# A new hand-set order for all five engine queues of a fused gated-attention and two-matrix feed-forward kernel

## The chip, the cores and the metric

The kernel runs on one core of one Trainium2 chip. The metric is device time in microseconds (us): the median over several executions. A profile is taken of one more execution; its own time stands beside its span, which runs from the first to the last instruction of the program.

## What is computed

The reference has two parts. The first is a gated linear attention over 4 batches, 8 heads, 768 tokens and 48 channels; the second is a feed-forward layer over the 3072 tokens with 384 channels in and out and 1024 inside.

```python
f = 1.0 / (1.0 + np.exp(-f_logit))
for t in range(S):
    state = f[:, :, t, :, None] * state + np.einsum('bhd,bhe->bhde', k[:, :, t], v[:, :, t])
    y[:, :, t] = np.einsum('bhd,bhde->bhe', q[:, :, t], state)
...
g = np.maximum(x @ w1, x @ w2)
return (g @ w_out).astype(np.float32)
```

Inputs and the output are float32. The kernel multiplies in bfloat16 and uses max(h1, h2) = relu(h1 - h2) + h2, so that the output is relu(x (w1 - w2)) w_out + x (w2 w_out).

## The kernel before

The work is cut into 12 spans of 256 tokens: span s is window s // 4 of batch s % 4, so spans s and s + 4 of one batch hang together through the state. Two neighbouring tokens share a partition, and a span is two chunks of 64 partitions.

Nothing schedules the kernel but a list written out by hand, ORDER. It has one word for each step. A word is a letter for the step, the span (and a part after the point), a letter for the engine where there is a choice (a ScalarE = ACT, v or w VectorE = DVE, p GpSimd = POOL, s SyncE = SP) and, after @, the PSUM bank that the step writes or reads (some steps take two banks, that one and the next). The loop at the end of the kernel emits the steps in the order of the list; each engine runs its own words in that order and waits where a word needs another's result, a free bank or a free buffer. The words, with the lines of their instructions:

- L (L115), W (L126, L130): loads by SP. The inputs of a span are four transfers (f, k, q, v) into slots of a pool of 25; Wa, Wb and Wo bring w1, w2 and w_out in halves into slots that are reused for inputs later.
- E, F, G (L192, L196, L200; ACT): the gate's exponentials and logarithm. e (L203): the sum over a token pair. C (L207, L210; TensorE = PE): running sums. X, Z (L217, L222; ACT): their exponentials. i, j (L226, L230): k and q of the even tokens. K, Q (L237, L240): the scaled k and q in bfloat16. V (a copy, L104): v in bfloat16.
- t, u (L257; PE): transposes of K's and Q's result. U (L104): their copy out of PSUM. A (L274; PE): products of k and q; m (L282; DVE): the same under the mask. D (L358; PE): what a span adds to the state; n, N (L375 to L380): the state's update. S (L314; PE): the part of y that comes from the first chunk's state; z (L330): a small read behind it; y (L314, L342; PE): the rest of y; Y (L104): its copy to bfloat16.
- d (L398; PE): x (w1 - w2), six products of 128x128 by 128x256 for each word. r (L407 on ACT, L409 on DVE): relu. o (L424; PE): the output product, eleven products of 128x128 by 128x384. b (L104): its copy out of PSUM into the tile ob. O (L442): the store of a span in one transfer of 384 KB; P (L436): of a part of it.
- ws (L485): w1 - w2 by quarters; wc (L104), wt (L459; PE), wx (L104): cast, transpose and copy of w2 by quarters; wo (L104): cast of w_out by quarters; wm (L475; PE): the product w2 w_out in three parts, wn (L104): its copy.

PE uses three tile shapes: 64x64 in A, S, y and D, 64x128 in t and u, 128x128 in all others. Counted along ORDER, neighbouring PE words differ in shape 64 times.

Of the kernel before, what the change touches and what calls it, by code (L numbers as in the profile page):

```python
# [17 lines left out]


ORDER = """  # L20
Lf0s@12 Lk0s@13 Lq0s@14 Lv0s@15 E0 Lf1s@16 F0 G0 e0v Lk1s@12 i0v C0@0 j0v X0 Lq1s@17 Z0 K0v V0a Q0v
t0@0 Lv1s@13 u0@0 E1 D0@2 Wb0s U0v@0 F1 n0.0v A0.0@0 e1p G1 Wa0s n0.1v S0@4 Wb1s A0.1@2 z0 Wa1s i1p
m0.0v@0 C1@6 Wo0s Z1 Wo1s j1v X1 V1a K1v Lf2s@16 Q1v t1@6 wc0a m0.1v@2 u1@6 D1@0 wc1a U1v@6 y0 n1.0v
n1.1v A1.0@6 Y0a@4 N1.1w S1@2 ws0p m1.0v@6 A1.1@0 wt0@4 z1 m1.1v@0 wt1@5 Lf3s@17 ws1p wx0a@4 d0.0@6
wx1a@5 y1 wc3v d0.1@7 wc2v Y1v@2 wt2@5 r0.0a@6 wt3@4 ws2v d1.0@2 Lq2s@0 ws3p d1.1@3 wx2v@5 d1.2@6
Lk2s@1 wx3v@4 d0.2@0 r1.0v@2 wo2a wo3p d0.3@1 Lv2s@2 wo0a wo1p d1.3@7 r0.1v@0 E2 wm0@2 Lk3s@8 F2
r1.1v@6 wm2@3 E3 e2p Lq3s@16 G2 C2@6 F3 j2v wm1@7 Lv3s@17 wn2a@3 e3v X2 C3@3 Z2 i2v o0.0@0 wn0a@2
Lf4s@9 K2v wn1a@7 V2a Q2v oz0.0@0 t2@6 Lf5s@1 X3 D2@4 N0.1v G3 u2@6 n2.0v o1.0@2 b0.0a@0 i3p U2v@6
Lk4s@0 n2.1v j3v A2.0@6 Lq5s@2 b1.0a@2 A2.1@4 K3p o0.1@0 m2.0v@6 Z3 V3a Lv4s@10 m2.1v@4 S2@6 E4 D3@2
z2 Q3v Lq4s@8 t3@4 F4 y2 u3@4 G4 e4p Lk5s@16 o1.1@1 b0.1a@0 U3v@4 Y2a@6 i4p E5 n3.0v Lf7s@9 n3.1v  # L30
C4@0 b1.1v@1 d2.0@4 X4 Z4 A3.0@2 K4p Lv5s@1 A3.1@6 F5 d2.1@5 m3.0v@2 G5 d2.2@0 Lk7s@17 r2.0a@4
m3.1v@6 e5p S3@2 d2.3@1 V4a z3 C5@4 j4v Lq7s@0 y3 X5 Q4v Z5 t4@6 Y3a@2 D4@4 r2.1v@0 N2.1p Lf6s@10
u4@6 i5p d3.0@2 n4.0v d3.2@0 U4v@6 Lf8s@8 d3.1@3 j5v d3.3@1 r3.0a@2 N4.0w Lk6s@11 N3.1p o2.0@6 n4.1v
K5v E7 Lq11s@3 r3.1a@0 Q5v t5@2 A4.0@4 b2.0a@6 V5p A4.1@0 u5@2 m4.0v@4 Lq6s@2 o2.1@6 U5a@2 m4.1v@0
O0s Lv7s@1 D5@4 F7 A5.0@0 S4@2 n5.0v o3.0@7 Lk9s@9 m5.0v@0 e7p G7 E6 N5.0p z4 b2.1v@6 Lv6s@16 F6
n5.1v y4 N4.1v G6 j7v A5.1@4 S5@0 e6p Y4a@2 o3.1@6 m5.1v@4 Lf9s@10 z5 i7v j6v C6@4 C7@5 Lq9s@6
b3.0v@7 X6 d4.0@2 i6p Z7 b3.1v@6 y5 X7 K6v Z6 O1s d4.1@3 Lk8s@7 Y5a@0 K7v d4.2@4 r4.0a@2 Lv11s@11
Q6v d5.0@0 V7a d4.3@5 Q7v t6@2 O3s r4.1a@4 t7@6 u6@2 u7@6 d5.1@1 U6v@2 O2s E8 d5.2@4 F8 U7v@6 D7@2
Lv8s@8 d5.3@5 r5.0a@0 e8p n7.0v o4.0@6 N7.0w E9 V6p Lv9s@0 n7.1v r5.1v@4 Lq8s@10 N5.1p A6.0@2
b4.0a@6 D6@0 m6.0v@2 A6.1@4 C8@6 o4.1@7 Z8 n6.0v X8 m6.1v@4 N6.0p Lf10s@16 G8 A7.0@2 n6.1v b4.1a@7  # L40
A7.1@4 S7@0 m7.0v@2 F9 Lk10s@1 o5.0@7 G9 N7.1v m7.1v@4 i9p Lf11s@2 o5.1@6 b5.0a@7 z7 O4s S6@4
b5.1a@6 y7 z6 e9v O5s y6 Lq10s@17 N6.1v Y7a@0 j8v C9@6 j9v Y6a@4 d7.0@0 Lk11s@4 i8v Z9 d7.2@2 Q8v
Lv10s@5 X9 d7.1@1 V8a K9v d6.0@6 r7.0a@0 d7.3@3 K8v d6.1@7 r7.1a@2 Q9v d6.2@0 E10 t9@4 r6.0v@6 t8@2
u9@4 F10 u8@2 d6.3@1 U8v@2 E11 o7.0@6 r6.1a@0 U9v@4 D8@7 b7.0a@6 A8.0@4 A9.0@0 n8.0v V9a A9.1@2
m8.0v@4 N8.0p o6.0@7 F11 m9.0v@0 G11 V11a o7.1@6 j11v b6.0a@7 m9.1v@2 e10p V10a D9@7 e11p A8.1@2
S8@0 n9.0v o6.1@4 m8.1v@2 z8 N9.0w j10v C10@7 S9@2 i11p Z10 y8 z9 b7.1v@6 Q10p y9 b6.1v@4 O7s Y8a@0
O6s C11@6 X10 Y9v@2 d8.2@0 X11 G10 d8.0@4 K11v Z11 d9.0@2 i10v d9.2@6 K10p d9.1@3 d8.1@5 r9.0a@2
d9.3@7 Q11p r8.0v@4 d8.3@1 r9.1a@6 t10@2 t11@4 u10@2 u11@4 o9.0@6 U10v@2 U11a@4 r8.1v@0 D11@7
b9.0a@6 A10.0@4 A11.0@2 n11.0v D10@6 m10.0v@4 N11.0p A11.1@0 o8.1@7 m11.0v@2 A10.1@4 n10.0v m11.1v@0
S11@2 N10.0p o8.0@6 z11 m10.1v@4 S10@0 y11 b8.0v@6 z10 y10 Y11a@2 o9.1@6 Y10a@0 d10.0@0 b9.1v@6  # L50
d10.2@2 b8.1v@7 O9s d10.1@1 O8s d10.3@3 r10.0a@0 d11.2@6 d11.0@4 r10.1a@2 d11.3@7 d11.1@5 o10.1@2
r11.0v@4 r11.1a@6 o10.0@3 o11.0@6 b10.0v@3 b10.1v@2 O10s o11.1@7 b11.0a@6 P11.0s o11.2@6 b11.1v@7
P11.1s b11.2a@6 P11.2a
"""


# [491 lines left out]
```

## Time and profile before

| what | value |
|---|---|
| median of 3 runs (lowest, highest) | 139.84 us (139.73, 140.19) |
| the profiled execution's own time | 139.43 us |
| its span | 137.6 us |
| granted clock of TensorE | 1.000 |
| DVE busy | 104.5 us, 165 instructions |
| ACT busy | 81.2 us, 120 instructions |
| POOL busy | 43.6 us, 53 instructions |
| moved by DMA | 28.68 MB, mean 208 GB/s |

The profile gives each engine's busy time, the span in 40 slices with the busy share of each in tenths, groups of instructions with their mean duration and the idle time before them, and the chain of work that ended last, followed back from the last instruction. The loads are spread over the first 92 us: SP issued the last one (v of span 10) at 89.46 us. PE's instructions can all be told apart by line, and since PE runs its words in the order of the list, every word's start and end can be read from the timeline: the first product of w2 and w_out (wm0) starts at 30.08 us, the last product of PE (o11.2) ends at 134.61 us.

### The profile page before, as it was taken

The numbers are of one execution on the slowest core, as the hardware profiler recorded it, in microseconds if no ns is written. First come the engines' busy times: TensorE is split into PE (matmuls) and PEld (weight loads), VectorE is DVE, ScalarE is ACT, GpSimd is POOL, SyncE is SP. The second block draws the span as 40 slices with busy tenths as digits, with TensorE's granted clock in tenths as the row PEclk, the third lists the DMA queues.
The fourth block names the chain that finished last, engine by engine and source line by source line (L and its number), as shares of the span: only waits on it lengthen the run. The fifth ranks groups of instructions, "written<-read, shape, count | busy, mean of one in ns | idle before, by whom it ended". The sixth has DMA issues, their size and how long they took to land.

```text
span 137.6 us, 5766 instructions
## 1 busy us (share of the span) xinstructions
PE 120.9 (88%) x2575; PEld 89.7 (65%) x2575; DVE 104.5 (76%) x165; ACT 81.2 (59%) x120; POOL 43.6 (32%) x53
## 2 busy tenths in 40 slices
PE   0047397999998999999999999999999999999991
PEld 0035286775656678666787667886678876778670
DVE  5778999995897799988969994988888379620330
ACT  3646564279847883898599554988717570226110
POOL 7604119542162587017104320002814902000000
PEclk9999999999999999999999999999999999999999
DMA  4999999999999999999998799994005000005023
GB/s 107 273 261 262 368 388 377 346 257 256 270 264 251 253 252 265 254 272 317 250 296 246 261 286 260 325 283 118 5 0 225 13 2 5 5 21 213 0 114 114
DMA packets 54617, 28.68 MB, mean 208 GB/s; under 512 B 50240, under 2 KB 51648, under 8 KB 54592
## 3 DMA queue, kind: packets, MB, share of 16 engines
q1 hardware_dynamic: 54448, 28.25, 77.8%
q8 instruction: 20, 0.33, 1.0%
q10 hardware_dynamic: 144, 0.07, 0.2%
q14 instruction: 5, 0.04, 0.1%
HBM read 23.59 MB, written 4.72 MB: 206 GB/s over the span
## 4 chain that ended last, share of the span: by engine, by line
PE 65%; DMA 13%; DVE 10%; SPq 3%; ACT 3%; issue 3%; DVEq 0%
PE banks L424 28%; PE banks L398 16%; DMA slots<-in_moe_w_out_dram 10%; PE banks L342 4%; PE banks L257 4%; PE banks L274 3%; PE banks L475 3%; DMA slots<-in_f_logit_dram 3%; PE banks L314 3%; DVE at_m L282 2%; DVE slots L230 2%; SPq L126 2%; PE banks L358 2%; PE banks L207 2%; DVE trs L104 2%
## 5 line engine op out<-in xcount | busy, mean ns | idle before, releaser
L424 PE MATMUL banks<-wo,gT 128*128 128x384 bf16 (+2 forms) x200 | 35.3, 320 | 0.0
L398 PE MATMUL banks<-xT,wd 128*128 128x256 bf16 x288 | 34.2, 273 | 1.0 <-POOL wd L485 0.8
L398 PEld LDWEIGHTS <-wd 128*128 128x128 bf16 x288 | 27.0, 98 | 5.3 <-POOL wd L485 1.1
L282 DVE TENSOR_TENSOR at_m<-banks,mask 128x1024 bf16<-128x1024 f32 x24 | 28.8, 1216 | 1.6 <-PE banks L274 1.4
L424 PEld LDWEIGHTS <-gT 128*128 128x128 bf16 x200 | 19.2, 98 | 11.9
L407 ACT ACTIVATE gT<-banks 128x1024 bf16<-128x1024 f32 x15 | 15.2, 1019 | 11.1 <-PE banks L398 10.4
L203 POOL TENSOR_TENSOR e<-ell 128x384 bf16<-128x384 f32 x9 | 9.1, 1019 | 27.1 <-ACT ell L196 21.0
L424 PE MATMUL banks<-m,xT 128*128 128x384 bf16 (+2 forms) x75 | 15.9, 321 | 0.0
L409 DVE TENSOR_SCALAR gT<-banks 128x1024 bf16<-128x1024 f32 x9 | 10.9, 1219 | 6.3 <-PE banks L398 6.3
L104 DVE COPY trs<-banks 128x2048 bf16<-128x2048 bf16 x10 | 12.0, 1220 | 4.6 <-PE banks L257 4.6
L104 ACT COPY ob<-banks 128x384 f32<-128x384 f32 (+2 forms) x15 | 7.5, 506 | 13.2 <-PE banks L424 12.5
L104 ACT CAST xT<-banks 128x768 bf16<-128x768 f32 x10 | 8.0, 800 | 9.0 <-PE banks L342 8.9
L104 DVE COPY ob<-banks 128x384 f32<-128x384 f32 (+2 forms) x14 | 7.2, 540 | 7.5 <-PE banks L424 5.5
L192 ACT ACTIVATE gate<-slots 128x768 f32<-128x768 f32 x12 | 10.0, 837 | 4.1 <-DMA slots<-in_f_logit_dram 4.1
L342 PE MATMUL banks<-at_m,vb 64*64 64x128 bf16 x576 | 11.6, 224 | 0.0
L380 POOL TENSOR_TENSOR st<-tmp_s,dec 128x192 bf16<-128x192 f32 x8 | 4.1, 510 | 20.7 <-PE banks L274 12.9
L274 PE MATMUL banks<-trs 48*64 48x128 bf16 x384 | 9.9, 230 | 0.8 <-DVE trs L104 0.8
L226 POOL TENSOR_TENSOR slots<-slots,one 128x384 f32<-128x384 f32 x7 | 8.0, 1145 | 7.6 <-ACT one L200 7.0
L196 ACT ACTIVATE ell<-gate 128x768 f32<-128x768 f32 x12 | 10.1, 843 | 0.5
L207 PE MATMUL banks<-e,u_inc 128*128 128x384 bf16 x12 | 4.2, 353 | 7.0 <-DVE e L203 6.8
L230 DVE SCALAR_TENSOR_TENSOR slots<-gate,slots 128x384 f32<-128x384 f32 x12 | 8.7, 732 | 1.7 <-DMA slots<-in_k_dram 1.4
L342 PEld LDWEIGHTS <-vb 64*64 64x64 bf16 x576 | 10.0, 111 | 0.0
...
## 6 DMA issues: line engine op xcount, KB each, us to landing
...
```

Of the source, the lines that this page charges most:

```text
L104: (nc.scalar.copy if e == "a" else engines[e].tensor_copy)(out, in_)
L192: nc.scalar.activation(flat(gate[s]), flat(loaded[s]["f"]), AF.Exp, bias=0.0, scale=-1.0)
L196: nc.scalar.activation(flat(ell[s]), flat(gate[s]), AF.Ln, bias=1.0, scale=1.0)
L203: engines[e].tensor_add(pad("e", s)[:, :, 0:D], ell[s][:, :, 0, :], ell[s][:, :, 1, :])
L230: engines[e].scalar_tensor_tensor(out=even, in0=gate[s][:, :, 1, :], scalar=1.0, in1=even, op0=ALU.add, op1=ALU.mult)
L274: nc.tensor.matmul(out=ps[h * HC:(h + 1) * HC, j % 2, par, :], lhsT=t[rows, h, 0, j, par, :], rhs=t[rows, h, 1, j].rearrange("p a t -> p ( ...
L282: nc.vector.tensor_mul(at[s][:, jj].rearrange("p r j a t -> p (r j) (a t)"), banks[:, b:b + 2, :].rearrange("p r (j x) -> p (r j) x", j=2) ...
L342: nc.tensor.matmul(out=ys[s][h][cols, kt, :], lhsT=window(vb[rows, par], head, off), rhs=m[rows, head // 4, head % 2, head // 2 % 2, par, ...
L398: nc.tensor.matmul(out=ps[:, f, :], lhsT=wd[:, kt, ff * C:(ff + 1) * C], rhs=x_flat(g)[:, kt, :], start=(kt == 0), stop=(kt == KT - 1))
L407: nc.scalar.activation(dst, src, AF.Relu)
L409: nc.vector.tensor_relu(dst, src)
L424: nc.tensor.matmul(out=ps, lhsT=x, rhs=w, start=(n == 0), stop=(n == KT + FG - 1))
```

## The change

Only ORDER changes. The words of the steps are the same but for stores and engines: all words of PE (177) stay, in another order, and neighbouring ones now differ in tile shape 56 times instead of 64 (9 instead of 8 times ahead of the product of w2 and w_out, 47 instead of 56 times from there on). Other words go to other engines, the largest shifts being: V to POOL 7 times (2 before), to DVE once and to ACT 4 times (10); U to ACT 4 times (2); b to ACT 19 times (13); K and Q to POOL 4 and 3 times (3 and 2); e to DVE 6 times (3); Y to DVE 4 times (2); two quarters of ws to DVE (one before), wc all to ACT (two before). Banks and slots are renumbered to fit. Spans 7 to 10 are stored in two transfers of 192 KB (P) instead of one of 384 KB (O); three of these halves are issued by ACT.

```diff
-Lf0s@12 Lk0s@13 Lq0s@14 Lv0s@15 E0 Lf1s@16 F0 G0 e0v Lk1s@12 i0v C0@0 j0v X0 Lq1s@17 Z0 K0v V0a Q0v
-t0@0 Lv1s@13 u0@0 E1 D0@2 Wb0s U0v@0 F1 n0.0v A0.0@0 e1p G1 Wa0s n0.1v S0@4 Wb1s A0.1@2 z0 Wa1s i1p
-m0.0v@0 C1@6 Wo0s Z1 Wo1s j1v X1 V1a K1v Lf2s@16 Q1v t1@6 wc0a m0.1v@2 u1@6 D1@0 wc1a U1v@6 y0 n1.0v
-n1.1v A1.0@6 Y0a@4 N1.1w S1@2 ws0p m1.0v@6 A1.1@0 wt0@4 z1 m1.1v@0 wt1@5 Lf3s@17 ws1p wx0a@4 d0.0@6
-wx1a@5 y1 wc3v d0.1@7 wc2v Y1v@2 wt2@5 r0.0a@6 wt3@4 ws2v d1.0@2 Lq2s@0 ws3p d1.1@3 wx2v@5 d1.2@6
-Lk2s@1 wx3v@4 d0.2@0 r1.0v@2 wo2a wo3p d0.3@1 Lv2s@2 wo0a wo1p d1.3@7 r0.1v@0 E2 wm0@2 Lk3s@8 F2
-r1.1v@6 wm2@3 E3 e2p Lq3s@16 G2 C2@6 F3 j2v wm1@7 Lv3s@17 wn2a@3 e3v X2 C3@3 Z2 i2v o0.0@0 wn0a@2
-Lf4s@9 K2v wn1a@7 V2a Q2v oz0.0@0 t2@6 Lf5s@1 X3 D2@4 N0.1v G3 u2@6 n2.0v o1.0@2 b0.0a@0 i3p U2v@6
-Lk4s@0 n2.1v j3v A2.0@6 Lq5s@2 b1.0a@2 A2.1@4 K3p o0.1@0 m2.0v@6 Z3 V3a Lv4s@10 m2.1v@4 S2@6 E4 D3@2
-z2 Q3v Lq4s@8 t3@4 F4 y2 u3@4 G4 e4p Lk5s@16 o1.1@1 b0.1a@0 U3v@4 Y2a@6 i4p E5 n3.0v Lf7s@9 n3.1v
-C4@0 b1.1v@1 d2.0@4 X4 Z4 A3.0@2 K4p Lv5s@1 A3.1@6 F5 d2.1@5 m3.0v@2 G5 d2.2@0 Lk7s@17 r2.0a@4
-m3.1v@6 e5p S3@2 d2.3@1 V4a z3 C5@4 j4v Lq7s@0 y3 X5 Q4v Z5 t4@6 Y3a@2 D4@4 r2.1v@0 N2.1p Lf6s@10
-u4@6 i5p d3.0@2 n4.0v d3.2@0 U4v@6 Lf8s@8 d3.1@3 j5v d3.3@1 r3.0a@2 N4.0w Lk6s@11 N3.1p o2.0@6 n4.1v
-K5v E7 Lq11s@3 r3.1a@0 Q5v t5@2 A4.0@4 b2.0a@6 V5p A4.1@0 u5@2 m4.0v@4 Lq6s@2 o2.1@6 U5a@2 m4.1v@0
-O0s Lv7s@1 D5@4 F7 A5.0@0 S4@2 n5.0v o3.0@7 Lk9s@9 m5.0v@0 e7p G7 E6 N5.0p z4 b2.1v@6 Lv6s@16 F6
-n5.1v y4 N4.1v G6 j7v A5.1@4 S5@0 e6p Y4a@2 o3.1@6 m5.1v@4 Lf9s@10 z5 i7v j6v C6@4 C7@5 Lq9s@6
-b3.0v@7 X6 d4.0@2 i6p Z7 b3.1v@6 y5 X7 K6v Z6 O1s d4.1@3 Lk8s@7 Y5a@0 K7v d4.2@4 r4.0a@2 Lv11s@11
-Q6v d5.0@0 V7a d4.3@5 Q7v t6@2 O3s r4.1a@4 t7@6 u6@2 u7@6 d5.1@1 U6v@2 O2s E8 d5.2@4 F8 U7v@6 D7@2
-Lv8s@8 d5.3@5 r5.0a@0 e8p n7.0v o4.0@6 N7.0w E9 V6p Lv9s@0 n7.1v r5.1v@4 Lq8s@10 N5.1p A6.0@2
-b4.0a@6 D6@0 m6.0v@2 A6.1@4 C8@6 o4.1@7 Z8 n6.0v X8 m6.1v@4 N6.0p Lf10s@16 G8 A7.0@2 n6.1v b4.1a@7
-A7.1@4 S7@0 m7.0v@2 F9 Lk10s@1 o5.0@7 G9 N7.1v m7.1v@4 i9p Lf11s@2 o5.1@6 b5.0a@7 z7 O4s S6@4
-b5.1a@6 y7 z6 e9v O5s y6 Lq10s@17 N6.1v Y7a@0 j8v C9@6 j9v Y6a@4 d7.0@0 Lk11s@4 i8v Z9 d7.2@2 Q8v
-Lv10s@5 X9 d7.1@1 V8a K9v d6.0@6 r7.0a@0 d7.3@3 K8v d6.1@7 r7.1a@2 Q9v d6.2@0 E10 t9@4 r6.0v@6 t8@2
-u9@4 F10 u8@2 d6.3@1 U8v@2 E11 o7.0@6 r6.1a@0 U9v@4 D8@7 b7.0a@6 A8.0@4 A9.0@0 n8.0v V9a A9.1@2
-m8.0v@4 N8.0p o6.0@7 F11 m9.0v@0 G11 V11a o7.1@6 j11v b6.0a@7 m9.1v@2 e10p V10a D9@7 e11p A8.1@2
-S8@0 n9.0v o6.1@4 m8.1v@2 z8 N9.0w j10v C10@7 S9@2 i11p Z10 y8 z9 b7.1v@6 Q10p y9 b6.1v@4 O7s Y8a@0
-O6s C11@6 X10 Y9v@2 d8.2@0 X11 G10 d8.0@4 K11v Z11 d9.0@2 i10v d9.2@6 K10p d9.1@3 d8.1@5 r9.0a@2
-d9.3@7 Q11p r8.0v@4 d8.3@1 r9.1a@6 t10@2 t11@4 u10@2 u11@4 o9.0@6 U10v@2 U11a@4 r8.1v@0 D11@7
-b9.0a@6 A10.0@4 A11.0@2 n11.0v D10@6 m10.0v@4 N11.0p A11.1@0 o8.1@7 m11.0v@2 A10.1@4 n10.0v m11.1v@0
-S11@2 N10.0p o8.0@6 z11 m10.1v@4 S10@0 y11 b8.0v@6 z10 y10 Y11a@2 o9.1@6 Y10a@0 d10.0@0 b9.1v@6
-d10.2@2 b8.1v@7 O9s d10.1@1 O8s d10.3@3 r10.0a@0 d11.2@6 d11.0@4 r10.1a@2 d11.3@7 d11.1@5 o10.1@2
-r11.0v@4 r11.1a@6 o10.0@3 o11.0@6 b10.0v@3 b10.1v@2 O10s o11.1@7 b11.0a@6 P11.0s o11.2@6 b11.1v@7
-P11.1s b11.2a@6 P11.2a
+Lf0s@12 Lk0s@13 Lq0s@14 Lv0s@15 E0 Lf1s@16 F0 e0v G0 Lk1s@12 i0v C0@0 j0v X0 Lq1s@17 Z0 K0v Q0v t0@2
+Lv1s@13 V0p u0@2 E1 U0v@2 Wb0s D0@0 F1 n0.0v e1p G1 Wa0s S0@2 n0.1v Wb1s A0.0@4 z0 Wa1s i1p C1@0
+m0.0v@4 Wo0s A0.1@6 X1 Wo1s Z1 m0.1v@6 Lf2s@16 K1v y0 j1v wc0a Q1v t1@6 V1a u1@6 Y0a@2 D1@0 U1v@6
+wc1a n1.0v ws0p A1.1@6 A1.0@2 n1.1v S1@4 m1.0v@2 wt1@0 wt0@1 Lk2s@13 ws1p z1 d0.0@2 m1.1v@6 wc3a
+wc2a wx0v@1 wt3@6 d0.1@3 wx1v@0 ws2v y1 r0.0a@2 ws3v d0.2@0 Y1a@4 Lq2s@0 wt2@7 wo0p wo1a d1.2@4
+wx2a@7 d1.0@2 N0.1p Lf3s@8 d0.3@1 wx3v@6 d1.1@3 wo2a wo3p Lv2s@9 d1.3@5 r1.0v@2 wm2@6 E2 r0.1v@0
+Lk3s@10 F2 wm0@7 e2v G2 Lv3s@16 wn2a@6 i2p C2@0 wm1@1 Z2 X2 j2v Lq3s@11 wn0a@7 K2v o0.0@0 wn1a@1 E3
+Q2v Lf4s@13 F3 oz0.0@0 t2@6 N1.1v u2@6 G3 e3p o0.1@1 Lk4s@0 U2v@6 r1.1a@4 V2p b0.0a@0 Lf5s@8 C3@0
+i3p b0.1a@1 A2.0@6 D2@4 X3 m2.0v@6 A2.1@2 V3a o1.0@1 K3p Lq4s@9 Z3 n2.0v m2.1v@2 Lq5s@16 S2@6
+b1.0a@1 z2 j3v y2 E4 Q3v Lv4s@10 D3@2 Y2a@6 t3@0 n2.1v u3@0 n3.0v F4 d2.2@6 n3.1v Lf6s@11 d2.0@2 G4
+e4v E5 U3v@0 i4p C4@4 d2.1@3 Lk5s@13 X4 d2.3@7 r2.0a@2 K4v o1.1@5 Lq6s@8 Z4 j4v r2.1a@6 Q4v t4@2
+Lf7s@0 F5 b1.1v@5 A3.0@6 A3.1@0 N2.1v u4@2 m3.0v@6 e5p o2.0@5 U4a@2 O0s Lv5s@9 V4p m3.1v@0 Lk6s@2
+C5@4 G5 S3@2 A4.0@0 b2.0a@5 z3 D4@6 j5v X5 y3 n4.0v Z5 O1s N4.0w o2.1@5 E6 Q5p n4.1v Y3v@2 Lq7s@10
+F6 m4.0v@0 d3.2@2 i5p b2.1a@5 Lk7s@16 E7 d3.0@6 K5p A4.1@0 F7 S4@4 Lv6s@0 d3.1@7 m4.1v@0 d3.3@3
+r3.0a@6 N4.1p z4 t5@0 e7v y4 r3.1a@2 N3.1p Lf9s@13 e6p u5@0 C7@6 U5v@0 o3.0@7 Z7 X7 Lv7s@11 Y4v@4 G6
+V5a i6p A5.0@0 b3.0v@7 A5.1@4 Lv10s@3 G7 D5@2 m5.0v@0 C6@7 o3.1@6 X6 Z6 Lv8s@9 K6p m5.1v@4 d4.2@0
+n5.0v b3.1a@6 Lv9s@6 N5.0w V6a d4.0@4 n5.1v S5@6 N5.1v D6@2 z5 j6v Lf8s@0 y5 Q6v d4.1@5 Y5a@6 n6.0v
+Lk8s@2 d4.3@1 N6.0w r4.0a@4 i7v d5.0@6 j7v r4.1a@0 d5.2@4 Lq9s@8 n6.1v K7v d5.1@7 E9 d5.3@5 Q7v O2s
+r5.0a@6 Lq8s@13 t6@0 t7@2 V7p u6@0 u7@2 U6v@0 o4.0@6 Lk9s@10 U7a@2 r5.1v@4 Lf11s@11 D7@0 F9 A6.0@2
+n7.0v A6.1@4 o4.1@7 m6.0v@2 b4.0a@6 N7.0p E8 e9p n7.1v Lk11s@0 m6.1v@4 C9@6 b4.1a@7 A7.0@0 A7.1@2 F8
+m7.0v@0 S6@4 O3s o5.0@7 Lk10s@16 G8 V9v Z9 X9 Lq11s@7 j9v o5.1@6 z6 m7.1v@2 b5.0a@7 G9 Lf10s@6 e8v
+S7@2 i8p b5.1a@6 y6 z7 i9v y7 Y6a@4 K9v O4s C8@6 Y7a@2 d6.0@4 Q9v Z8 d6.2@0 X8 d6.1@5 K8v d7.0@6
+r6.0a@4 j8v d6.3@1 E11 Q8p d7.1@7 r6.1v@0 d7.2@4 F11 t8@2 r7.0v@6 G11 t9@0 N6.1p u8@2 u9@0 V8p
+d7.3@5 U8v@2 U9a@0 o6.0@6 r7.1v@4 j11v A8.0@2 b6.0a@6 D9@7 i11v D8@4 E10 A9.0@0 n8.0v o7.0@6 N8.0v
+m8.0v@2 e11p n9.0v o7.1@4 b7.0a@6 m9.0v@0 N9.0p F10 P7.0s Lq10s@6 G10 O5s A9.1@0 b7.1v@4 S9@6 A8.1@2
+e10v C11@5 P7.1a o6.1@4 z9 m9.1v@0 X11 Z11 K11p m8.1v@2 S8@0 b6.1a@4 y9 z8 O6s Q11p y8 Lv11s@0 Y9a@6
+C10@2 Y8v@0 d9.0@6 X10 i10p Z10 d9.2@4 d9.1@7 j10v K10v d9.3@5 r9.0a@6 d8.0@0 Q10v r9.1a@4 t11@6
+t10@2 u11@6 V11p u10@2 U11v@6 d8.2@4 U10a@2 N7.1p d8.1@1 V10p d8.3@5 r8.0a@0 o9.1@2 r8.1a@4 A11.0@0
+A10.0@4 m11.0v@0 D11@3 o9.0@6 n11.0v m10.0v@4 N11.0p D10@3 b9.0a@6 A11.1@0 n10.0v A10.1@4 P9.0a
+S11@6 m11.1v@0 N10.0p o8.0@3 z11 m10.1v@4 S10@0 b8.0a@3 y11 z10 P8.0s y10 o8.1@3 Y10v@0 b9.1v@2
+P9.1s d10.0@0 b8.1a@3 d10.2@4 P8.1a Y11a@6 d10.1@1 d10.3@5 r10.0v@0 d11.0@6 d11.2@2 r10.1a@4 d11.1@7
+o10.1@4 r11.0v@6 d11.3@3 o10.0@5 r11.1a@2 o11.0@2 b10.0v@5 b10.1a@4 P10.0s o11.1@3 b11.0a@2 P11.0s
+P10.1s o11.2@2 b11.1v@3 P11.1s b11.2a@2 P11.2a
 """
```

## The prediction

> **What bounds the kernel now.** First the page: which engine is full, and when.
>
> ```profile
> PE 120.9 (88%) x2575; PEld 89.7 (65%) x2575; DVE 104.5 (76%) x165; ACT 81.2 (59%) x120; POOL 43.6 (32%) x53
> ...
> PE   0047397999998999999999999999999999999991
> ...
> DVE  5778999995897799988969994988888379620330
> ```
>
> PE has no idle slice from the tenth on; DVE is full in slices 5 to 9 (13 to 31 us) and eases towards the end. Then the chain that ended last:
>
> ```profile
> 14.22 14.22 DMA slots<-in_moe_w_out_dram
> ...
> 28.46 1.57 ACT wo L104 x2
> 30.04 0.04 issue
> 30.08 2.76 PE banks L475 x16
> ...
> 39.22 1.36 DVE slots L230
> 40.58 2.28 DVE at_m L282 x2
> 42.86 0.04 issue
> 42.90 0.41 PE banks L257 x16
> ...
> 68.55 2.73 PE banks L398 x24
> 71.28 1.04 PE banks L257 x64
> ...
> 122.20 5.24 PE banks L398 x48
> 127.44 7.19 PE banks L424 x55
> ```
>
> To 28.4 us the weights arrive; two casts of w_out on ACT follow and release wm0 at 30.08. From there to 134.61 PE runs almost without a break: 104.53 us. So the sum is this: when the product w2 w_out starts, what PE's work costs after it, what PE waits for after it, and the tail of 137.6 - 134.6 = 3.0 us.
>
> **When the product starts.** Before it, PE has the same words in both orders, and the loads up to Wo1 keep their order, so w_out again lands at 28.44 (estimate from that row). Now only one of its casts stands on ACT behind this landing (wo2a; wo3p runs beside it on POOL, 0.83 us by its group): 29.3 is the earliest, 0.8 before 30.08. PE itself sets a later point. I followed DVE's queue with the durations of before: A0.1 now comes behind C1, which waits for e1p (13.24), so m0.1 ends near 15.5, K1 16.4, Q1 17.9, U1 19.8 (18.95 before, so 0.8 later), m1.0 22.2, m1.1 23.5, wx0 and wx1 24.5. Off DVE go wc2, wc3 and Y1 (0.94 + 0.94 + 0.95); onto it comes a second quarter of ws. What that costs no row shows directly, so it gets two bounds.
>
> ```profile
> 24.28 1.81 POOL L485 TENSOR_TENSOR wd<-slots 128x768 bf16<-128x768 f32 x1 [0.47 <-DMA slots<-in_moe_w_dram]
> 24.92 1.98 DVE L485 TENSOR_TENSOR wd<-slots 128x768 bf16<-128x768 f32 x1
> ...
> 39.13 1.44 DVE L230 SCALAR_TENSOR_TENSOR slots<-gate,slots 128x384 f32<-128x384 f32 x1
> ```
>
> The one quarter on DVE took 1.98 us while POOL did another. Word j, also with two SBUF inputs, takes 0.56 alone and took 1.44 at 39.13 while K3p held POOL until 40.17: such an instruction seems to wait for POOL. K on DVE, as many float32 elements from two SBUF inputs, takes 0.953. In the new order POOL is idle from 23.8 until wo0p, so I take 0.95 for each of ws2 and ws3 (the nearest row), 1.98 as the other end. Then ws2 ends at 25.4 and ws3 at 26.35; y1 ends at 25.6, and behind it PE needs five d in a row after d0.2, with wt2 between: 6 x 0.655 + 0.34 = 4.3, the product starts at 29.9. **Gain 0.2** (ends: 0.8 gained, 0.8 lost with 1.98 twice).
>
> **PE's work after it.** The words are the same, but changes of shape fall from 56 to 47. What one costs: eight d in a row take 5.24, 0.655 each; four d ahead of a transpose take 2.73 - 4 x 0.655 = 0.11 more; an output product takes 1.79 ahead of another (7.19 holds three of them and two parts of a fourth, of 1.20 and 0.6) and 1.89 ahead of a 64-row step. Read so at all pairs, a change costs 0.09 to 0.11, say 0.10. **Gain 9 x 0.10 = 0.9** (nothing at the least, if the drain of the array overlaps otherwise in the new neighbourhoods).
>
> **What PE waits for after it.** Before, three waits can be read: t3 started at 42.90 where D3's products (0.37) were through at 42.30, because the masks m2 (until 42.84) stood behind j3, which K3p held up: 0.60; C2 waited 0.12 for e2, t5 0.12 for K5. Sum 0.84, and all three places are rearranged: j3 now stands behind both m2.
>
> For the new order I laid PE's words from 29.9 on with the steps above and looked, word by word, when the result or the bank it needs is there, by the durations of the groups (U 1.22 on DVE, 1.87 on ACT, m 1.22, r 1.02 and 1.22, K and Q 0.95 and 1.82, V 0.83, Y 0.80 and 0.95, b 0.48 and 0.55). Loads land in their order, every 1.53 us for 384 KB (24 loads between 26.5 and 63.2 us before). Where a result is late:
> - y2 0.2 (m2.1 ends at 41.8), u3 0.15 (Q3 at 43.4), d2.2 0.1 (Y2 at 43.8), C4 0.1 (F4, then e4, at 45.2);
> - A3.0 and A4.0 0.15 together (relu of span 2 on ACT; mask of span 3);
> - A5.1 and D5 0.2 (Y4 behind U5 on DVE; V5 on ACT at 63.3);
> - u7 0.35: DVE has j6, Q6, n6, N6, i7, j7, n6, K7, Q7 from 67 on, some 6.2 us, and V7p falls between, so Q7 ends at 73.6 where PE stands at 73.3;
> - S6 and S7 0.2 (masks of 6 and 7).
>
> Sum 1.35. The rest has cover. U4, U9 and U10, moved to ACT at 0.65 more each, end within 0.2 of their readers (S3, A9.0, o9.1): any delay of ACT there goes onto PE. V on POOL is ready 1 us or more before D reads it. DVE has some 22 us of work in the 26 us between U2 and Y4, against 22.8 of 25 before at 35 to 60: it has become looser. **Loss 1.35 - 0.84 = 0.5.** The ends: no loss but a gain of 0.8, if my small waits vanish; a loss of 1.5, if each is twice as long.
>
> **Stores and SP.** P7.0 waits on SP for b7.0 (96.7) with Lq10 and O5 behind it; Lq10 lands near 98.5 and is read by j10 near 104, so the cover is 5 us. Lv11 goes out behind O6 near 101.5 and is needed by D11 at 112. P7.1a and P8.1a stand on ACT ahead of X11 and Y11: an issue of 0.37 (the row of P11.2) and, for P8.1a, the wait for o8.1, so Y11 comes at 123.0 and d11.0 reads it at 123.8: 0.8 of cover. At the end P10.1 goes out behind P11.0, where before O10 had left at 132.15: some 192 KB more are in flight when the last part (64 KB, 1.6 us) leaves. **Loss 0.1** (0 to 0.7, the time of 192 KB at the mean of 250 to 290 GB/s).
>
> **Sum.** -0.2 - 0.9 + 0.5 + 0.1 = -0.5. Against the profiled execution's 139.43 this gives 138.9; the median of the runs lies 0.4 above that execution, and 139.84 - 0.5 = 139.3. Timed runs decide, so I take a value just under it: **139.2**.
>
> **Rivals.**
> - *The waits vanish.* Most of mine are 0.05 to 0.2, below what rows of mean durations can settle. With PE's words back to back the time is 139.84 - 0.2 - 0.9 - 0.8 + 0.1 = 138.0. For it: PE before kept a pace with 0.84 of waits in 104 us. Against it: u7 and y2 hang on sums of whole queues. Chance 0.20.
> - *ws at full price.* If a DVE quarter of ws costs 1.98 without POOL beside it, ws3 ends at 28.4, the product starts at 30.9, and 1.0 of the gain goes: 140.2 against 139.2, no change. DVE's K at 0.953 speaks against it. Chance 0.12.
> - *Slower: DVE is held up by POOL.* The change gives POOL five more V, one more K and one more Q. In the profile, whichever of the two starts first holds the other: j3 +0.88 behind K3p, j5 +0.57 beside V5p, i5 on POOL 1.71 instead of 1.00 beside Q4. In the new order V7p, Q8p and i8p stand beside DVE's i, j, K and Q ahead of u7 and u8, and V2p, i3p and K3p beside j2 and e3. It decides from the point where it meets a queue without slack: at u7 each such hit of 0.8 goes to PE whole, at u8 (Q8p ends at 90.8, PE reads at 90.9) too, and around u3 the slack is gone already. Three hits, 2.4 us, give 139.2 + 2.4 = 141.6; two give 140.8. For it: no slack at these three places; against it: POOL's words stand mostly beside words that read PSUM, which the rows show undisturbed (U2 1.22 beside K3p). Chance 0.26, most of it near 140.8.
>
> [...]
>
> That the fewer changes of shape save nothing would give 140.1, no change; the pairs above leave it a chance of 0.05, and it goes with the second rival.
>
> **Chances.** A measurement of this kernel tells some 0.3% (0.42 us) from no change. The forecast with 138.5 to 139.7 has 0.37, most of it faster (0.32) and the rest within; the first rival 0.20, faster; second rival and shape 0.17, of which 0.13 within and 0.04 slower; the slower rival 0.26. So faster 0.52, same 0.18, slower 0.30. The range runs from 138.0 (first rival) to 141.0 (two hits and a little more); the forecast's own is 138.5 to 139.7.
>
> **What would show it.** ws on DVE twice near 0.95; the first L475 at 29.9; PE unbroken behind it, in 47 changes, with its longest waits at t, u and y of spans 2 and 3 and at u7; the last product near 134.1. I am wrong if ws costs 2 us, if j, i, K or Q on DVE are stretched over 1 us in many places, or if PE waits for U on ACT.

## The result and the profile after

The changed kernel takes **141.95 us** (median of 5, 141.51 to 143.18) against 140.00 for the kernel before, measured beside it (median of 5, 139.73 to 140.19): ratio 1.0155, 95% interval 1.012 to 1.019. It is 1.6% slower, where 139.2 was predicted, and lies outside the predicted range. A second measurement (after_timed, below) gave 1.0136 [1.0094, 1.0178].

The page of the profiled execution (143.18 us, the longest of the five; span 141.1):

```profile
span 141.1 us, 5779 instructions
...
PE 123.6 (88%) x2575; PEld 92.6 (66%) x2575; DVE 98.5 (70%) x158; ACT 83.2 (59%) x122; POOL 48.1 (34%) x58
...
PE   0046769999999999996999999999998999999992
...
PEclk9999999999999999999999999999999999999999
```

PE has the same 2575 products as before, but is busy 2.7 us longer (123.6 against 120.9), and DVE's busy time has fallen by 6.0. So some products have become slower, which no added wait does. The row of the granted clock shows nines throughout, as in the kernel before, but it is no witness for the first 20 to 26 us: the packed trace records the granted clock in stretches, the first of them starts at 20.02 us in the profile of before and at 26.41 in that of after, and where nothing is recorded the page prints full clock.

The chain that ended last, with the lines that answer to those of before:

```profile
23.00 1.28 PE banks L398 x6
...
24.92 1.28 PE banks L398 x6
...
31.64 2.60 PE banks L475 x16
...
65.00 1.10 issue
...
105.58 0.93 issue
...
132.96 5.41 PE banks L424 x44
...
138.38 0.27 ACT ob L104
```

Three things differ. Six products of 128x128 by 128x256 (one word d) take 1.28 us, where a word d in a row of eight took 0.655 before; PE's share of the chain now starts long before the product w2 w_out, which comes at 31.5 instead of 30.1; and between PE's words stand two pieces called "issue", 1.10 and 0.93, in which PE waited for nothing that the profile knows.

| | before | after | difference |
|---|---|---|---|
| start of the product w2 w_out (first L475) | 30.08 | 31.48 | +1.40 |
| from there to the end of the last product | 104.53 | 106.87 | +2.34 |
| from there to the end of the span | 3.0 | 2.7 | -0.3 |
| span | 137.6 | 141.1 | +3.5 |

In the profile of after_timed (141.16 us, nearer to the median; the run is described below) the first row is 31.41 and the second 104.94, and between PE's words no such piece is over 0.3 us.

**The pace before the product.** The same 12 us in both profiles, each engine's busy time, before first:

```profile
20.00:26.00 6.00, 5.22 (x116) 4.29 (x113) 6.00 (x8) 2.90 (x4) 5.31 (x3) 1.00 1.06 378
26.00:32.00 6.00, 5.39 (x43) 3.89 (x41) 5.32 (x6) 3.51 (x5) 1.94 (x4) 1.00 1.17 276
```

and after (columns: length, PE, PEld, DVE, ACT, POOL with their instructions, granted clock, DMA share, GB/s):

```profile
20.00:26.00 6.00, 5.78 (x68) 4.70 (x68) 5.38 (x10) 1.63 (x3) 3.58 (x2) 1.00 1.06 378
26.00:32.00 6.00, 6.00 (x101) 5.19 (x101) 1.86 (x3) 5.63 (x8) 2.13 (x3) 1.00 1.11 264
```

From 20 to 26 us PE was busier after, and did 68 products where it had done 116. PE's timeline shows where the pace changes; first before, then after (start, duration, engine, line, operation, tiles, shape, count, idle time ahead):

```profile
16.74 0.61 PE L257 MATMUL banks<-ident,qp 64*128 64x64 bf16 x16 [0.26 <-DVE qp L240]
...
20.48 0.84 PE L459 MATMUL banks<-ident,w2b 128*128 128x128 bf16 x12
22.08 0.83 PE L398 MATMUL banks<-xT,wd 128*128 128x256 bf16 x6 [0.76 <-POOL wd L485]
```

```profile
15.89 1.49 PE L342 MATMUL banks<-at_m,vb 64*64 64x128 bf16 x46 [0.91 <-DVE at_m L282]
...
18.29 0.61 PE L257 MATMUL banks<-ident,qp 64*128 64x64 bf16 x16 [0.38 <-DVE qp L240]
...
20.22 1.07 PE L274 MATMUL banks<-trs 48*64 48x128 bf16 x32 [0.76 <-DVE trs L104]
...
21.54 1.46 PE L459 MATMUL banks<-ident,w2b 128*128 128x128 bf16 x12
22.79 1.49 PE L398 MATMUL banks<-xT,wd 128*128 128x256 bf16 x6
...
26.36 0.80 PE L342 MATMUL banks<-at_m,vb 64*64 64x128 bf16 x40
```

Twelve transposes of w2 took 0.84 us before and 1.46 after; six products of d took 0.83 and 1.49. Small products show where the pace changes: one of A (L274) goes from 0.31 to 0.21 us at 20.1 before, one of y (L342) from 0.31 to 0.22 at 26.3 after. These are the places at which the trace's record of full clock begins (20.02 and 26.41). In what follows, "half pace" is the stretch ahead of that point. Before, PE had been busy without a gap from 16.74, some 3.4 us, when full pace came. After, it waited three times in the same stretch (0.91 us until 15.89, 0.38 until 18.29, 0.76 until 20.22), and full pace came only 6.1 us after the last of these.

**The pieces of "issue".** They stand in the middle of one word, between two instructions of one kind:

```profile
64.78 0.22 PE L358 MATMUL banks<-vb,kp 64*64 64x48 bf16 x7
66.10 0.38 PE L358 MATMUL banks<-vb,kp 64*64 64x48 bf16 x25 [1.10 <-issue]
```

```profile
105.35 0.23 PE L314 MATMUL banks<-trs,st 48*64 48x128 bf16 x4
106.50 0.31 PE L314 MATMUL banks<-trs,st 48*64 48x128 bf16 x8 [0.93 <-issue]
```

Counting weight loads and products from the start, the first break stands ahead of instruction 2240 and the second ahead of 4032: they lie 1792 instructions, 7 x 256, apart, and both counts leave 192 over when divided by 256. The page lists 20 transfers on the instruction queue (q8), 0.33 MB, so 16 KB each; PE's 5150 products and weight loads make 20 blocks of 256. In the trace one of these transfers ends 1.45 us before PE goes on at 66.10 (at 64.65) and one 1.24 us before 106.50 (at 105.26). PE had gone through the 256 instructions ahead of the breaks in 3.96 and 3.85 us. In the profile of before, the fetch of a block always ended at least 1.53 us ahead of its first use.

### The profile page after: what moved, and what is told of

It reads as the page before. It is cut to its first block, busy times and chain, and to the rows that moved or that the text cites. A ratio compares the mean times of both kernels' runs of the same rounds, so it can differ in the third digit from the quotient of the medians.

```text
span 141.1 us, 5779 instructions
## 1 busy us (share of the span) xinstructions
PE 123.6 (88%) x2575; PEld 92.6 (66%) x2575; DVE 98.5 (70%) x158; ACT 83.2 (59%) x122; POOL 48.1 (34%) x58
## 4 chain that ended last, share of the span: by engine, by line
PE 75%; DVE 9%; issue 6%; DMA 4%; POOL 2%; SPq 2%; ACT 1%; DVEq 0%; ACTq 0%; POOLq 0%
PE banks L424 25%; PE banks L398 24%; PE banks L342 5%; PE banks L257 5%; PE banks L274 4%; DVE at_m L282 4%; DMA slots<-in_v_dram 4%; PE banks L314 4%; PE banks L475 3%; PE banks L207 2%; PE banks L459 2%; SPq L115 2%; PE banks L358 1%; DVE slots L230 1%; POOL vb L104 1%
## 5 line engine op out<-in xcount | busy, mean ns | idle before, releaser
L398 PE MATMUL banks<-xT,wd 128*128 128x256 bf16 x288 | 35.4, 279 | 0.0
L398 PEld LDWEIGHTS <-wd 128*128 128x128 bf16 x288 | 28.0, 100 | 4.3
L424 PEld LDWEIGHTS <-gT 128*128 128x128 bf16 x200 | 19.3, 98 | 12.0
L104 ACT COPY ob<-banks 128x384 f32<-128x384 f32 (+2 forms) x20 | 9.7, 483 | 20.9 <-PE banks L424 20.9
L409 DVE TENSOR_SCALAR gT<-banks 128x1024 bf16<-128x1024 f32 x8 | 9.6, 1220 | 8.6 <-PE banks L398 4.4
L104 DVE COPY trs<-banks 128x2048 bf16<-128x2048 bf16 x8 | 9.8, 1222 | 5.8 <-PE banks L257 5.8
L342 PE MATMUL banks<-at_m,vb 64*64 64x128 bf16 x576 | 12.0, 225 | 0.9 <-DVE at_m L282 0.9
L380 POOL TENSOR_TENSOR st<-tmp_s,dec 128x192 bf16<-128x192 f32 x9 | 4.9, 547 | 20.1 <-DVE tmp_s L375 20.1
L274 PE MATMUL banks<-trs 48*64 48x128 bf16 x384 | 10.2, 235 | 1.0 <-DVE trs L104 0.8
L342 PEld LDWEIGHTS <-vb 64*64 64x64 bf16 x576 | 10.3, 112 | 1.2 <-issue 1.2
L314 PE MATMUL banks<-trs,st 48*64 48x128 bf16 x240 | 8.8, 228 | 2.3 <-issue 0.9
L217 ACT ACTIVATE inv<-banks 128x384 f32<-128x384 f32 x12 | 5.9, 490 | 6.3 <-PE banks L210 5.2
L203 POOL TENSOR_TENSOR e<-ell 128x384 bf16<-128x384 f32 x6 | 6.0, 998 | 9.6 <-ACT ell L196 9.6
L237 POOL TENSOR_TENSOR kp<-slots,inv 128x768 bf16<-128x768 f32 x4 | 7.3, 1813 | 5.8 <-ACT inv L217 5.7
```

Of the source, the lines that this page charges most:

```text
L104: (nc.scalar.copy if e == "a" else engines[e].tensor_copy)(out, in_)
L274: nc.tensor.matmul(out=ps[h * HC:(h + 1) * HC, j % 2, par, :], lhsT=t[rows, h, 0, j, par, :], rhs=t[rows, h, 1, j].rearrange("p a t -> p ( ...
L314: nc.tensor.matmul(out=ys[s][h][cols, kt, :], lhsT=window(state_before(s, h)[rows], head // 2, off), rhs=tr[s][rows, h, 1, head // 2].rear ...
L342: nc.tensor.matmul(out=ys[s][h][cols, kt, :], lhsT=window(vb[rows, par], head, off), rhs=m[rows, head // 4, head % 2, head // 2 % 2, par, ...
L398: nc.tensor.matmul(out=ps[:, f, :], lhsT=wd[:, kt, ff * C:(ff + 1) * C], rhs=x_flat(g)[:, kt, :], start=(kt == 0), stop=(kt == KT - 1))
L409: nc.vector.tensor_relu(dst, src)
```

## The experiments

Theory: (1) PE runs at half pace until it has been busy without a gap for long enough, and the new order's waits between 15 and 20 us put that off; (2) PE stands when a block of 256 instructions is used up before the next has been fetched. Rivals: DVE and POOL hold each other up, as the prediction's slower case had it; the transfers alone slow PE. Products that are added in a run (h: identity times mask, 128x128 by 128x256, six a word of six; g: pairs of 64x64 products) are extra work whose result nobody reads. Ratios are to before, measured beside.

**The changed kernel once more, and timed.**

> The changed kernel once more, for a second profile. Theory 1 (PE runs at half pace until 26 us because its busy stretch is broken by waits): again d0.0 and d0.1 near 1.3 to 1.4 us for six products instead of 0.66, and the first product of w2 and w_out near 31.5 us. Theory 2 (PE stands still where its next block of 256 instructions has not come in): breaks of about 1 us, if they occur, at the same instruction counts, 2241 and 4033 of PE's own weight loads and products; the lag of a fetch varies, so one of the two may be missing, and the span is then 1 us shorter. Rival (the breaks are noise of one execution): breaks at other counts or none.

> The changed kernel unchanged, timed beside the others of this call. Theory 1: half pace until 25 to 27 us. Theory 2: a break at instruction 4033, sometimes one at 2241; a median of 141.3 to 142.0 with a spread of over 1 us from the number of breaks.

after_again (one execution): 141.45 us, product w2 w_out at 31.33, half pace to 26.2, a break of 0.62 us ahead of instruction 4032 again, none at 2240. after_timed: 141.94 (9 executions, 140.96 to 143.04), half pace to 26.1, and only 0.29 us lost ahead of 4032. So the pace is the same in each profile; the break at 4032 is in all three with 0.29 to 0.93 us, and the one at 2240 in one.

**Filling the waits** (after_warm).

```diff
-A0.1@6 X1 ... t1@6 V1a u1@6 Y0a@2 D1@0
+A0.1@6 h6@5 X1 ... t1@6 h2@5 V1a u1@6 Y0a@2 D1@0 h4@5
```

> The changed kernel with twelve more products on PE (identity by mask, into a free bank, their result read by nobody) in the places where PE stood between 14.5 and 20.2 us. Theory 1: PE comes to full pace before the first d; d0.0 takes 0.66 to 0.75, not 1.28, and the first product of w2 and w_out starts at 29.9 to 30.3 us instead of 31.5; 1.2 to 1.6 us off the time. Rival (something else than pace slows PE there, a shared memory port or the arrival of weights): d0.0 stays at 1.3 and the time too. Theory 2: the 24 more instructions move the block ends; a break near 65 us may stay, that near 105 us may go.

139.37 us (10 executions), ratio 0.9964 [0.9939, 0.9989] (the interval in brackets, here and below, is the 95% one): 2.6 us less than the changed kernel by *added* work. PE's timeline:

```profile
13.36 0.48 PE L207 MATMUL banks<-e,u_inc 128*128 128x384 bf16 x1 [0.36 <-POOL e L203]
...
14.42 1.46 PE L489 MATMUL banks<-mask,ident 128*128 128x256 bf16 x6
...
17.47 0.41 PE L257 MATMUL banks<-ident,kp 64*128 64x64 bf16 x16
```

From 13.36 PE has no gap, and at 17.3 the transposes take 0.41 us for 16 where they took 0.63 at 18.29 in the profile of after. The record of full clock begins at 17.31. The product w2 w_out starts at 29.78, some 1.6 us earlier than in the changed kernel. The 24 added instructions also move the ends of the blocks, and the largest break left in the profile is 0.34 us; that leaves some 1 us of the 2.6 for the breaks.

**The same products in the old order** (before_warm: eight behind C1, one behind t1).

> Control: the kernel before with nine added products in its early waits (eight behind C1, one behind t1). Theory 1: full pace some 3 us earlier, about 17 us, but the first product of w2 and w_out hangs on the landing of w_out and its casts there, so it stays at 29.7 to 30.1 and the time within 0.4 us of the kernel before. Rival (added products make any order of this kernel faster, so that they do not mend the change): 1 us or more below the kernel before.

140.36, ratio 1.0011 [0.9977, 1.0046]: nothing. Full pace comes at 19.3 instead of 20.1, but PE then waits 0.34 us for a copy and 0.71 ahead of the first word d, and loses 0.82 to a break of the kind above, ahead of instruction 703 (191 over):

```profile
25.48 0.61 PE L398 MATMUL banks<-xT,wd 128*128 128x256 bf16 x4 [0.82 <-issue]
```

The product starts at 30.53, later than expected. The last cast of w_out on ACT, which it needs, ended at 30.42, so without the break it would not have started much earlier. So filling helped where pace was late (after_warm) and not where data was (here).

**The early order of PE, both ways** (after_y0late, before_y0early).

```diff
 after_y0late
-m0.1v@6 ... y0 ... t1@6 V1a u1@6 Y0a@2 D1@0 U1v@6
+m0.1v@6 t1@4 V1a u1@4 D1@0 y0 U1v@4 Y0a@2
 before_y0early
-C1@6 ... t1@6 wc0a m0.1v@2 ... y0
+C1@6 m0.1v@2 ... y0 t1@6 wc0a
```

> The changed kernel with one move undone: the mask m0.1 behind Q1 on DVE and y0 behind D1 on PE, as in the kernel before (t1 and u1 go to banks 4 and 5 for it). Theory 1 (the move of y0 opened the wait for U1 and so kept PE at half pace): PE reaches full pace by about 20 to 21 us, d0.0 takes under 0.8 us of its own, the first product of w2 and w_out starts at 29.7 to 30.3 us, time 1.2 to 1.6 us below the changed kernel. Rival (the pace hangs on when the first d starts): as the changed kernel, 31.4. Theory 2: breaks at 4033, perhaps 2241, stay.

> The kernel before with that move alone: m0.1 ahead of j1 on DVE and y0 ahead of t1 on PE. Theory 1: PE's stretch is now broken by the wait for U1; half pace lasts to 23 to 27 us, the first product of w2 and w_out starts 0.5 to 1.4 us later than 30.08, time 0.5 to 1.4 us above the kernel before. Rival (the move does not matter, something else of the change slows PE's start): no change.

after_y0late missed its expectation: 142.93, ratio 1.0213 [1.0152, 1.0274], half pace to 26.5, product at 32.14. Only a part of the old order was put back, and D1 now met a wait that y0 had covered:

```profile
18.60 0.63 PE L358 MATMUL banks<-vb,kp 64*64 64x48 bf16 x32 [0.94 <-ACT vb L104]
```

V1 stands on ACT behind wc0. The break ahead of 4032 stayed, with 0.81 us. before_y0early came out in the expected direction, but by less: half pace to 24.9, the product at 30.49, 140.29, ratio 1.0035 [1.0013, 1.0057]. Its profile is no clean proof of the move of y0: a break of 0.44 us ahead of instruction 447 (191 over) fell into the same stretch, at 18.85, beside the wait of 0.17 us at 20.47.

**The early order whole** (after_pre, then after_early).

```diff
 after_pre
-A0.0@4 ... C1@0 m0.0v@4 Wo0s A0.1@6 X1 Wo1s Z1 m0.1v@6 Lf2s@16 K1v y0 j1v wc0a Q1v t1@6 V1a u1@6 Y0a@2 D1@0 U1v@6
+A0.0@4 ... A0.1@6 C1@0 m0.0v@4 Wo0s X1 Wo1s Z1 Lf2s@16 j1v V1a K1v wc0a Q1v m0.1v@6 t1@4 u1@4 D1@0 y0 U1v@4 Y0a@2
 after_early: after_pre, with S0 y0 Y0 in bank 4, A0.0 t1 u1 U1 in bank 2, and the edit of after_lq10 (below)
```

> The changed kernel with its early order put back as far as PE's stretch goes: A0.1 ahead of C1, j1 ahead of K1, V1 on ACT ahead of wc0, m0.1 behind Q1 and y0 behind D1. The trial with m0.1 and y0 alone had left V1 behind wc0, D1 at 18.6 us and PE with waits of 1 us on both sides. Theory 1: no wait over 0.4 us from 15.9 us to U1, full pace by 20 to 21 us, the first product of w2 and w_out at 29.6 to 30.2, time 1.2 to 1.7 us below the changed kernel of this call. Rival (the later start comes from the number of words on ACT and DVE, not from the pace): still 31 or later. Theory 2: the break at 4033 stays.

> The early order of before is put back as in the kernel before it (A0.1 ahead of C1, j1 ahead of K1, V1 ahead of wc0, m0.1 behind Q1, y0 behind D1), now with S0, y0 and S1 in bank 4 and t1, u1, A1.0 in bank 2, so that A1.0 no longer waits for Y0's copy; q of span 10 goes early into its free slot and O5 ahead of P7.0. No work is added. Pace theory: PE is filled from 15.8 to past 19.3, reaches full pace near 20, the product starts at 29.8 to 30.2, no break at count 4033, span about 137.8, time 139.3 to 139.8. Rival (the half pace comes from something else in the new order, its transfers or its casts): half pace stays to 25 or 26, the product starts at 30.7 to 31.3, time 140.4 to 140.8.

after_pre: 141.65, ratio 1.0122 [1.0044, 1.0201], against an expectation of some 140.5. Up to 19.2 us PE is where it was before, within 0.1 us, and then A1.0 needs the bank that Y0 is still reading:

```profile
20.38 0.64 PE L274 MATMUL banks<-trs 48*64 48x128 bf16 x16 [0.47 <-ACT xT L104]
```

Half pace lasts to 25.0, the product starts at 30.70, and the break ahead of 4032 stayed, as expected, with 0.90 us. after_early has other banks and no such wait, and still:

```profile
20.94 1.46 PE L459 MATMUL banks<-ident,w2b 128*128 128x128 bf16 x12 [0.21 <-ACT w2b L104]
22.26 1.46 PE L398 MATMUL banks<-xT,wd 128*128 128x256 bf16 x6
```

PE was busy from 16.52 to 20.73, 4.2 us without a gap, then waited 0.21, and was slow to 24.9. The expectation of 20 us was wrong for this execution, and the product came at 30.53. As a time, 140.02 (10 executions, 139.28 to 141.33), ratio 0.9999 [0.9959, 1.0038], between what the pace theory and its rival had named: what the new order had lost is back, with no added work, but two edits share in it, the early order and that of after_lq10, which takes the break at 4032 away.

So "3.4 us without a gap" is not the rule. Taken from the end of PE's last gap of over 0.15 us, full pace came after 3.3 to 3.4 us (before, before_warm), 4.0 (after_warm, after_early), 4.4 (before_y0early), 4.6 (after_pre), 4.8 (after_y0late) and 5.8 to 6.2 us (the changed kernel, three times); after 5.8 in after_best, after 3.2 and, a second time, 6.7 in after_warm48, and between 4.7 and 6.1 in the four profiles not named; and in after_early 4.2 us once were not enough.

In the traces, though not on the pages, the record of the granted clock consists of whole steps of 3.41 us: full clock for 119.47 us (35 steps) from 20.02 in before, for 116.05 (34) from 26.41 in after, for 112.64 (33) from 26.10 in after_timed. The values above, 3.2 to 6.7 us, are 0.94 to 1.96 of these steps, and the 4.2 us that were not enough in after_early are 1.23. What decides how much time without a gap an execution needs is not shown. In each of the 15 profiles that have a record (after_early has none), the first full stretch begins within 0.2 us of the place at which the durations halve. What the clock was ahead of it is not recorded; that it was half is read from after_warm48, where PE had the pace, lost it and got it again. There the record reads 1.0 for one step from 16.46, 0.5 for two steps from 19.88, and 1.0 from 26.70 on, and the products in the half stretch take as long as in the slow stretch of the changed kernel (first line: the window, PE's busy time and then the other engines', granted clock, DMA share, GB/s):

```profile
19.90:26.60 6.70, 6.58 (x101) 5.34 (x101) 4.58 (x8) 3.16 (x5) 3.70 (x3) 0.50 1.06 374
```

```profile
22.86 1.46 PE L459 MATMUL banks<-ident,w2b 128*128 128x128 bf16 x12
24.11 1.49 PE L398 MATMUL banks<-xT,wd 128*128 128x256 bf16 x6
```

That a longer stretch without a gap makes full pace surer has only the spread of times for it, which the breaks widen too: after_warm, with 6.2 us without a gap, lies within 139.25 and 139.62 in nine of ten executions, while after_lq10 and after_early spread over 2.5 and 2.0 us.

**Moving the ends of the blocks** (24 or 72 pairs ahead of everything, where PE idles: 48 or 144 instructions).

```diff
-Lf0s@12 Lk0s@13
+g24@6 Lf0s@12 Lk0s@13
```

> The changed kernel with 24 small pairs of weight load and product ahead of everything, at about 3 us where PE has nothing to do: the ends of PE's blocks of 256 instructions move by 48 words, to places where no block is used up in less than 4.5 us. Theory 2: no break of 1 us anywhere behind 30 us, span 1 to 2.3 us below the 141.1 of the changed kernel's profile, median 0.5 to 2 us below 141.95. Rival (noise, or the breaks hang on the words D5 and y8 themselves): breaks stay at D5 and y8. Theory 1: the first product of w2 and w_out stays at 31.5.

> The same with 72 pairs, 144 instructions: now two blocks, at 103 and at 119 us, are used up in some 1.9 and 2.3 us. Theory 2: breaks of 1.5 to 3 us in or right behind y9, y8 and y11, y10, the time 2 to 4 us above that of the kernel with 48. Rival: the same time as with 48.

> Before, with 72 small pairs of products (144 PE instructions whose result nobody reads) ahead of everything, where PE has nothing to do: every block of 256 instructions ends 144 instructions earlier along the list. Fetch theory: the old order has no break only because its blocks end at good words; now some end in stretches that use a block up in about 2 us, so one or two breaks of 0.8 to 1.3 us appear, at counts that leave 192 over by 256, near 102 or 118 us, and the time is 1 to 2 us above before: 141 to 142. Rival (the breaks belong to the new order and its transfers): no gap over 0.6 us behind 30 us that no other engine explains, time 139.9 to 140.4.

after_shift48: 140.65, ratio 1.0047 [1.0016, 1.0079]; no break behind 30 us, half pace to 25.8. after_shift144 (2 executions): 143.22, 1.0249 [1.0189, 1.0308]; breaks ahead of instructions 1472 and 4288, in words that had none:

```profile
44.70 0.38 PE L257 MATMUL banks<-ident,kp 64*128 64x64 bf16 x14
46.07 0.20 PE L257 MATMUL banks<-ident,kp 64*128 64x64 bf16 x2 [0.99 <-issue]
```

before_shift144, the old order, which has no such break of its own: 143.11 (2 executions), 1.0212 [1.009, 1.0335], breaks ahead of 704, 3520 (0.50) and 4288:

```profile
22.91 0.22 PE L459 MATMUL banks<-ident,w2b 128*128 128x128 bf16 x1 [1.04 <-issue]
...
106.81 0.32 PE L207 MATMUL banks<-e,u_inc 128*128 128x384 bf16 x1 [1.46 <-DVE xT L104]
```

The last line names a copy on DVE, because it ended last; before, the same product began right behind y9, ahead of that copy. All these counts leave 192 over by 256, and PE goes on 1.2 to 1.6 us after the block has landed, in each of these seven breaks (two in after, two here, three in the old order); the two of before_warm and before_y0early fit, with 1.5 us and a count one lower. Behind the added pairs nothing but the places of the blocks' ends was changed in either order, and the breaks moved with them, so the fetch is the cause. Most crossings cost next to nothing: in the profile of after, PE stood for 1.10 and 0.93 us at 2 of 20 ends of blocks and under 0.1 at each of the others; the longest wait in these runs is the 1.46 us above. In the seven breaks the block ahead had lasted 1.9 to 4.3 us; in before_warm and before_y0early 5.4 and 5.8, but there the fetch had begun only 3.9 us after PE had entered that block.

**The transfers ahead of the late fetch** (after_lq10).

```diff
-Lf10s@6 ... F10 P7.0s Lq10s@6 G10 O5s
+Lf10s@6 Lq10s@14 ... F10 O5s P7.0s G10
```

> The changed kernel with the load of q of span 10 (into a slot that is free all along) and the store of span 5 issued ahead of P7.0 instead of behind it, so that they leave near 90 us and not at 100 to 102. Theory 2 in its narrow form (the fetch at 101.5 to 105.3 came late because these transfers filled the DMA rings): the break at instruction 4033 shrinks by 0.5 us or goes; that at 2241 may stay. Rival (a fetch takes that long anyhow, the block is just used up too fast): the break at 4033 stays at 0.8 to 1.1 us. In either case 0 to 1 us below the changed kernel.

140.55, ratio 1.0045 [1.0009, 1.0082], 1.4 us less than the changed kernel, with no word of PE moved. q of span 10 goes out early instead of behind P7.0; in the profile of after, P7.0, this load and O5, 960 KB together, were issued at 100.25, 100.70 and 101.14, just ahead of the late fetch. The place of the second break:

```profile
104.40 0.34 PE L314 MATMUL banks<-trs,st 48*64 48x128 bf16 x12
```

These are twelve products in one piece. The fetch of this block began 0.4 us after PE had entered the block ahead and landed 2.6 us before its use (in after_early 0.6 and 2.3); in the five profiles of the new order that have neither this edit nor added products it began 0.9 to 2.8 us after and landed 1.2 to 1.4 us before, with a loss each time (0.29 to 0.93 us). The break at 65.00 is absent too, as in after_again, so not all of the 1.4 us need be the edit's. By what means the transfers hold up a fetch (full rings, in the expectation) is not shown. Half pace stays to 26 us.

**Both together** (after_warm48: after_warm with 12 pairs at the start; after_best: after_warm with the edit of after_lq10 and D3 ahead of y2).

> The changed kernel with the twelve added products that fill PE's early waits, and twelve small pairs ahead of everything, 48 instructions in all, so that PE is at pace early and no block is used up in under 4.5 us. If both theories hold and add up: the first product of w2 and w_out at 29.8, no break behind it, not the 0.5 us ahead of D5 that the kernel with the twelve alone shows, span 137.0, time 138.7 to 139.2. If only pace matters: the same as with the twelve alone, 139.4.

> All that helped together: the twelve added products, the early load of q of span 10 with the store of span 5, and D3 ahead of y2, so that the wait of y2 for z2 (0.42 us) is filled. If the three add up: the first product at 29.8, no break at 4033, 0.3 us less ahead of y2, a time of 138.6 to 139.2, below the kernel before by 0.5 to 1%. Rival (breaks and the pace shift to other places): 139.4 or more.

Both missed the times that were expected if everything adds up. after_warm48: 139.88, 1.0015 [0.9979, 1.0051], in two groups (five at 139.25 to 139.53, five at 140.24 to 141.67). Its profile is of the longest execution: D1 waited 1.54 us for V1 on ACT, and the pace was lost again at 19.9. V1 stands behind wc0, and wc0 waited for the transfer of w2 until 18.40 (17.00 in after_warm); why that landed later is open. after_best: 139.37, 0.9965 [0.9935, 0.9995], the same as after_warm: the word D3 ahead of y2 moved the wait behind S2 and removed little of it (1.71 us from S2 to t3 instead of 1.81).

## Why the prediction was wrong

- **When the product starts: the step that failed.** "... behind it PE needs five d in a row after d0.2, with wt2 between: 6 x 0.655 + 0.34 = 4.3" held, from y1's end at 27.2 to 31.5. What failed is "y1 ends 25.6": I walked DVE's queue to that point and took PE's words by durations of a PE at full pace, though U1's lateness, which I had worked out (0.8 us; 1.2 measured), leaves PE idle just where it has to get its pace. The cost of that idle time stood in the sum at nothing. The stretch from 20.22 to 26.13 us holds 32 products of A, S1, 18 transposes and 12 products of d, some 3.2 us at the later rows' durations; they took 5.9. Predicted 29.9, measured 31.48; with the pace held (after_warm) 29.78.
- **ws on DVE: right, and for the reason given.** 0.948 and 0.949 us, where 0.95 was taken and 1.98 kept as the other end; POOL stood idle beside both. In the groups of after:

```profile
L485 DVE TENSOR_TENSOR wd<-slots x2: 948/948/949, 24.7 to 25.5; 128x768 bf16<-128x768 f32 x2
```

- **Shape changes: right as far as it can be read.** d ahead of d takes 0.655 and ahead of another shape 0.75 in both profiles, an output product 1.79 and 1.88 to 1.89. No run tested it alone, and what in the array costs the 0.10 is not shown.
- **What PE waits for after it: mis-sized.** 1.35 was predicted (the places listed there add up to 1.45, so that the loss and the time should have read 0.1 more). Against words back to back with 0.10 for each change of shape, some 4.76 us were lost in the profile of after (before: 1.56, where I had read 0.84). Of these some 2.41 are the two breaks; the fetch of instructions had no term in the sum. The other 2.35 have other places than mine: u7 (0.35 predicted) waited for nothing; y2 lost 0.42, y5 0.25, A10.1 0.46. The wait of y2, on DVE and on PE:

```profile
42.18 1.21 DVE L282 TENSOR_TENSOR at_m<-banks,mask 128x1024 bf16<-128x1024 f32 x1
43.45 0.16 DVE L330 COPY look<-banks 128x1 f32<-128x1 f32 x1
```

```profile
43.66 0.24 PE L314 MATMUL banks<-trs,st 48*64 48x128 bf16 x2 [0.25 <-DVE look L330]
```

  I had it as a late mask (0.2). The mask was there at 43.39, but y2 comes right behind S2 and so waits for DVE's small read of S2's result. The sum closes, with the 0.10 taken from the prediction: 4.76 - 1.56 - 9 x 0.10 = 2.3, measured 2.34.
- **Stores and SP: half right.** P7.0 held up q of span 10 and O5 without harm to j10, but the burst behind it lies on the fetch of a block of PE's instructions (after_lq10). The tail was 0.3 shorter, not 0.1 longer.
- **The slower rival: right in sign, wrong in mechanism.** j9 on DVE (from 83.54) and i8 on POOL (from 83.30), side by side, took 1.36 instead of 0.55 and 1.18 instead of 1.00, and PE lost 0.2 at S7; u7 and u8, which were to decide, did not wait. That the time came near what it named (140.8 to 141.6) has other causes: it is luck.

Median against median: pace some 1.3, waits 0.4 net of the shapes (after_timed's 31.41 and 104.94 against 30.08 and 104.53), the tail -0.3, and breaks of some 0.3 to 2 us by the execution, of which the 0.4 holds the smallest; 1.95 was measured.
